# A planned order of work on one core, searched anew with measured costs, and its last weight loads without gates

## The chip, the core and the metric

The kernel runs on one core of a Trainium2 chip. The core has a matrix engine (TensorE, in the profile PE, with its weight loader PEld), a vector engine (VectorE, DVE), an activation engine (ScalarE, ACT), a general engine (GpSimd, POOL) and a sync engine (SyncE, SP), which here only issues transfers; 16 DMA engines carry them out. The metric is the device time of one execution in microseconds (us); less is better.

## The reference

Two residual blocks are applied to x (2048 tokens x 576, bf16), and then the same two again with the same weights:

```python
x = x + A(layernorm(x))     # attention in segments, with a memory
x = x + B(layernorm(x))     # silu(x @ w1) * (x @ w3) @ w2, 576 -> 4608 -> 576
x = x + A(layernorm(x))
x = x + B(layernorm(x))
```

A goes through 64 segments of 32 tokens one after the other:

```python
for s in range(64):
    h = concat([mem, xs])                   # 8 memory rows and 32 tokens: 40 x 576
    q, k, v = h @ Wq, h @ Wk, h @ Wv        # 32 heads of 128
    p = softmax(mask(q @ k.T * 128 ** -0.5))
    o = (p @ v) @ Wo                        # 40 x 576
    mem = o[:8]                             # the memory of the next segment
    outs.append(o[8:])
```

Segment s + 1 needs the first 8 rows of the output of segment s. This chain runs through all 64 segments in both layers.

## The kernel before, in words

**Steps.** Layer 1 runs 8 segments behind layer 0 (LAG = 8). The work falls into 72 steps: step t is segment t of layer 0 together with segment t - 8 of layer 1. In steps 8 to 63 both layers are there, and since they share the weights, one product serves both with 80 moving columns (2 x 40). In steps 0 to 7 and 64 to 71 only one layer is there, and the same product moves 40 columns. The feed-forward of a layer works on 4 segments (128 tokens) at a time, and its pieces are spread between the attention of the steps; for the last 4 segments of layer 1 it can only come after step 71.

**Pieces.** The work is cut into nodes. A node is a function that issues some instructions on one engine, with a cost (`dur`), a delay until its result can be read (`lat`), the nodes that it depends on (`deps`) and the buffers that it takes and gives back (`acq`, `rel`). `make_nodes` (L248) writes them all. The nodes of PE have a letter for each kind:

| letter | node | letter | node |
|---|---|---|---|
| Q, q | Q and K projection of some heads: main part (512 rows), tail (64 rows) | n, a, b | transposes of a layernorm's result |
| S | scores of 8 heads | p | POST: transposes attention's output back |
| T | transpose of the probabilities on PE (one-layer steps only) | F, f | feed-forward up (w1, w3): main, tail |
| P | probabilities times V | W, w | feed-forward down (w2), layer 0 and layer 1 |
| O, o | product with Wo: main, tail | V, v, X, x, G, g | value projections |
| m | transpose of the first memory | | |

For a group of 8 heads the chain is: Q, q; copies of the projection to QKT (L662 on ACT or L665 on DVE); S; on DVE and ACT mask, maximum, exponential and sum (SME, STAT); scaling into PB; the transpose to PTS; P; copy to OT; O, o. There are four such groups in a step. In steps with both layers the transpose from PB to PTS isn't done by PE but by a DMA that SP issues (node TR, `ptr_dma`, L1103, the rows `PTS<-PB`). In steps with one layer PE transposes (T) into a bank, and ACT or DVE copies the bank to PTS. There is one buffer of PTS, two of PB and of SME, four of QKT, eight banks.

**What sets the order.** PE's order is a string of letters that is written into the kernel: ORDER = FIRST + FOUR * 11 + LAST (L217 to L240), 3601 letters. FIRST holds steps 0 to 15, FOUR (208 letters) four steps with both layers, repeated eleven times, and LAST the rest. Each letter takes the next node of its kind. The order on the other engines (ACT, DVE, POOL, and SP's issues) comes from `plan` (L93 on): it goes through time with the nodes' costs, and whenever an engine is free it takes the ready node of the lowest `prio`. Evictions (kind AD) go to ACT or DVE, whichever the plan has free. The plan runs while the kernel is built; the chip only sees the result, a fixed order of instructions on each engine, and semaphores. A wrong cost in the plan can't break a dependency; it can put work in a poor place.

**Array modes.** PE runs a product on the whole array, on halves of rows or of columns, or on smaller parts. A node can permit several modes (`mode="full/col"`), and the plan chooses one so that the shape changes seldom. The helper `mm` (L659) issues a product in mode "col" as two products of 64 columns each.

**Loads.** All attention weights are in SBUF: W (Wq and Wk), WV, WO. Loads go out on SP (`dma`, L668), some small ones on ACT (`adma`, L671) and POOL (`swdma`, L674). Feed-forward weights come in pairs of pieces as they are used: W13 (two buffers) and W2C (two buffers). For the feed-forward behind step 71 there is another way: as soon as the last projections and values have been computed, W and WV are free, and `tail_load` (L741) puts the feed-forward weights into them, eight loads, each in two parts (one into W, 1.18 MB, one into WV, 0.59 MB). Loads 1 to 7 have a **gate** (L572): load 1 goes out only when PE has done O of group 1 in step 71, loads 2 to 7 only after O of group 3.

```python
gates = {1: me["WO1"], **{i: me[f"WO{NG - 1}"] for i in range(2, 8)}}
for i in range(8):
    g = gates.get(i)
    tail.append([load("tail", kb(128, c), s0 + o.tail_at + 0.01 * i, em.tail_load(i, what, g), deps=dep + [g])
                 for what, c, dep in ((0, 9 * 512, qk_done[i]), (1, 4 * 576, v_done))])
```

**Tiles that the change touches.** HT (L1355) holds the transposed input of a step, 128 partitions x 3 x 5 x 176 columns; YTS (L1368) holds attention's output for POST, 2 x 5 x 128 columns.

Of the kernel before, what the change touches and what calls it, by code (L numbers as in the profile page):

```python
# [33 lines left out]
PTR = 112  # L34

# [7 lines left out]
         "xr": 3, "xn": 2, "w13": 2, "w2": 2, "htt": 4}  # L43
# [14 lines left out]
def role(t):  # L58

    return (t - LAG) % 2  # L60
# [29 lines left out]
KINDS = {"m0tr": "m", "L0tr": "a", "L1tr": "b", "POST": "p", "Ftr": "n", "QK": "Q", "QKt": "q", "SC": "S", "TR": "T", "PV": "P",  # L90
# [121 lines left out]
def ewh(*ns):  # L212
# [5 lines left out]
    "maQqSQQvqqVSxXTqSPQSTOPXoTPOTPoOoOoQqqQvSSqVqQSQTPSTOPOToPToxPOOooQqqQSqvSaVQQSqTPSTPOOoTPoTPOOooQqqQSQSvqVQTSqX"  # L218
    "SPTPOTOPoToxPOOooQqqpQvSSVqnQfFSTFfqQPWSTOPFTOfPFTofoPOOooWQFfqqfFSQQSqqfFvVfTFSPQWTSFPXffOTFPOTOPWOooooaxQqqQSW"
    "FSQvfqTVfSFPQFTfqOPSWTOPFOTffoooPFOoWQqqvSQQSFfqVfSTWqFQFSPTfPOTWPoTOPOOooobQpvVqqqQQSnQqfxFSXqqfFQQQPSWFqqfQOfS"  # L220
# [6 lines left out]
    "QqqqqQppQQvVSSnnQFfqqQFqSfQQPFfqOwPoSWFffOPFWOowoPFOoFffqqQQQQqqWSwFSGgfqqQQQPQqqgWSSGFPFffggGGPwOFOPOOffooowoFv"  # L227
    "VqqqQQQWSFqfqqQQQSwWFPSFfqqfQQPwOSWFFPoffOOWPwOoooFfqqQQWaSqqQQQbSQqgqGSQPQqqgGSOPoGggOPGwOPooOo"
# [4 lines left out]
    "QPFSTOPofFTOPwTWPOOoooFfqfqQQSQSFvqfVfqFTQPSWwSTFPxXffTFPOOTWOPwOFooooFqffqQQSWwVvqfSQFfqTQPSWTwPOSFOTfFPwTOPWOo"  # L233
    "oooFqfqfFQQWSfqSFwvVQQTSqffPWwSTFFPOoTOWPoTwPOOoobQpqxqvVSnQXqfFSQTQSPFfqOoTSFfPTwPOOoofTFPFOowQfqqQSQSFvqfVTqfF"
    "PQTSwPSXffFTOOPwTOPFOooooFxqfQQqqSvVSQTQSFPfqfOTSPwoOTFPFTOPoofOowQQfqqFSSvVqQQSqTwPTSPOOFTofPTPOOooopfffFFFnwfw"
    "FFffFFwfFffFwffwFFFFffwFwfffFFFwffFFwfffFFww"
# [11 lines left out]
def make_nodes(em, nseg, pools, o=Opt, dma_bw=230e3, load_bw=345e3):  # L248
# [24 lines left out]
    def load(name, nbytes, prio, fn, deps=()):  # L273
        return node("DMA", nbytes / load_bw, fn, deps=deps, prio=prio, name=name, lat=2.0)

    ld_m0 = node("ACT", 0.1, em.load_m0(), prio=-90, name="m0", lat=2.5)
    ld_t = [load("ldt", kb(3 * R64, 4096), -10.0, em.load_tails(0)), node("ACT", 0.1, em.load_tails(1), prio=-120, name="ldt", lat=6.0)]
# [47 lines left out]
    vx_ev, last_v, pvs = {}, [], {}  # L325

    def v_nodes(name, t, k, prio, tail_at, emit, strips, deps, tail_deps, free):

# [1108 lines left out]
```

## Time and profile before

| | |
|---|---|
| median of 3 runs | 2654.93 us (2654.26 to 2665.12) |
| the profiled execution's own time | 2657.81 us |
| its span (first to last recorded instruction) | 2656.0 us |
| TensorE busy | 2578.3 us, 97% |
| VectorE, ScalarE, GpSimd busy | 75%, 47%, 13% |
| mean granted TensorE clock | 0.992 |
| DMA packets | 371.48 MB, mean 140 GB/s |
| largest group of matmuls | bank<-HT,W, 785.1 us, 23,040 of them |

The profile is of one execution. Rows of groups read: line, engine, operation, what it writes <- what it reads, partitions x elements and type, how many; after the first bar the busy time in us and the mean of one in ns; after the second the engine's idle time just ahead of them and what ended most of it. Rows of waits read: engine, tile and line that waited, what it waited for; then the total in us, how often, and the longest. Rows of the queue of SP read: start in us, length, queue, line, what is loaded, and how many were joined in the row. Since most instructions are issued by a few helpers (L659, L662, L665, L668), they are told apart by their tiles.

### The profile page before, as it was taken

The page shows a single profiled execution, that of the slowest core. Times are in us where ns is not written, and L with a number is a line of the kernel's source. Part 1 is how long each engine was busy: PE and PEld are TensorE (multiplying, and loading weights), DVE is VectorE, ACT ScalarE, POOL GpSimd, SP SyncE. Part 2 cuts the span into 40 slices and gives each one's busy share as a digit, 9 for nine tenths or more (in the row PEclk, how much of TensorE's full clock was granted, in tenths as well). Part 3 has the DMA queues.
Part 4 walks back from the last instruction along what each step waited for, and adds up shares of the span by engine and source line. Part 5 has one row for each costly group of instructions (what it writes and reads, how often), then busy time and mean ns, then how long its engine had stood idle before and what let it go on. Part 6 is the DMA issues. An engine that isn't in the chain of part 4 may idle for free.

```text
span 2656.0 us, 133410 instructions
## 1 busy us (share of the span) xinstructions
PE 2578.3 (97%) x59426; PEld 2216.6 (83%) x59426; DVE 2004.1 (75%) x5137; ACT 1242.3 (47%) x3495; POOL 335.2 (13%) x399
## 2 busy tenths in 40 slices
PE   6899999999999999999999999999999999999998
PEld 4788878888888888888888888888888888888887
DVE  4677777877787778778777877877787787777866
ACT  2555453444545444454544544454444445454443
POOL 1111111110101111010101101110110111011110
PEclk8899999999999999999999999999999999999999
DMA  9055746556554655555465555645565554554458
GB/s 322 4 153 150 182 101 152 128 131 157 117 141 108 152 135 126 155 128 139 109 143 134 138 146 125 146 106 151 122 147 139 132 140 106 129 139 131 130 155 244
DMA packets 690433, 371.48 MB, mean 140 GB/s; under 512 B 234328, under 2 KB 682592, under 8 KB 689216
## 3 DMA queue, kind: packets, MB, share of 16 engines
q1 hardware_dynamic: 686320, 355.08, 53.5%
q8 instruction: 464, 7.60, 1.2%
q0 software_dynamic: 3024, 6.93, 0.9%
q10 hardware_dynamic: 512, 0.94, 0.2%
q14 instruction: 113, 0.93, 0.1%
HBM read 306.72 MB, written 2.36 MB: 116 GB/s over the span
## 4 chain that ended last, share of the span: by engine, by line
PE 83%; DMA 9%; DVE 5%; ACT 1%; issue 1%; SPq 1%; POOL 0%; ACTq 0%; DVEq 0%; POOLq 0%
PE bank L659 83%; DMA PTS<-PB 5%; DMA W<-in_B_w_dram 1%; DMA W2C<-in_B_w_dram 1%; DVE STAT L665 1%; DMA WV<-in_A_Wv_dram 1%; DVE SME L665 1%; DVE PB L665 1%; SPq L668 1%; DVE V L665 0%; DMA W<-in_A_Wq_dram 0%; ACT V L662 0%; DVE XR L665 0%; DVE HTT L665 0%; DVE LNS L665 0%
## 5 line engine op out<-in xcount | busy, mean ns | idle before, releaser
L659 PEld LDWEIGHTS <-W 128*128 128x128 bf16 (+2 forms) x32464 | 1259.9, 100 | 118.1 <-issue 63.6
L659 PE MATMUL bank<-HT,W 128*128 128x80 bf16 (+3 forms) x23040 | 785.1, 197 | 16.1 <-issue 9.3
L659 PE MATMUL bank<-XTB,W 128*64 128x256 bf16 (+5 forms) x9424 | 658.9, 263 | 2.0 <-DMA W<-in_B_w_dram 2.0
L1093 POOL MEMSET PB<- 128x1024 bf16 x288 | 273.9, 951 | 1944.4 <-DMA PTS<-PB 1142.8
L662 ACT ACTIVATE QKT<-bank 128x256 bf16<-128x256 f32 (+4 forms) x1423 | 342.4, 320 | 246.4 <-PE bank L659 216.9
L659 PE MATMUL bank<-OT,WO 128*128 128x80 bf16 (+3 forms) x11520 | 421.2, 199 | 1.0 <-ACT OT L662 0.5
L662 ACT ACTIVATE V<-bank 64x512 bf16<-64x512 f32 (+1 forms) x605 | 339.6, 585 | 164.9 <-PE bank L659 158.4
L659 PEld LDWEIGHTS <-WO 128*128 128x128 bf16 (+1 forms) x11520 | 387.8, 102 | 34.0 <-issue 18.7
L659 PE MATMUL bank<-WV,HT 128*32 128x512 bf16 (+4 forms) x3768 | 370.4, 386 | 5.1 <-DMA WV<-in_A_Wv_dram 4.5
L659 PE MATMUL bank<-W2C,HTT 128*64 128x288 bf16 (+1 forms) x3216 | 321.8, 287 | 3.4 <-DMA W2C<-in_B_w_dram 2.8
L662 ACT ACTIVATE OT<-bank 128x320 bf16<-128x320 f32 x374 | 153.8, 437 | 313.2 <-PE bank L659 309.3
L665 DVE TENSOR_REDUCE STAT<-SME 104x8 f32<-104x320 f32 (+1 forms) x576 | 275.1, 478 | 27.9 <-ACT SME L662 22.3
L665 DVE TENSOR_TENSOR PB<-SME,STAT 40x128 bf16<-40x128 f32 (+4 forms) x912 | 275.4, 336 | 12.1 <-DVE STAT L665 0.4
L665 DVE SCALAR_TENSOR_TENSOR HTT<-HTT,bank 128x512 bf16<-128x512 bf16 (+1 forms) x324 | 201.5, 622 | 106.7 <-ACT HTT L662 103.7
L659 PEld LDWEIGHTS <-HT 128*32 128x32 bf16 (+4 forms) x3768 | 155.4, 100 | 145.2 <-issue 39.1
L659 PEld LDWEIGHTS <-HTT 128*64 128x64 bf16 (+1 forms) x3288 | 230.1, 105 | 40.8 <-issue 7.3
L662 ACT ACTIVATE HTT<-bank 128x512 bf16<-128x512 f32 (+1 forms) x324 | 173.9, 548 | 179.9 <-PE bank L659 178.3
L665 DVE SCALAR_TENSOR_TENSOR XR<-bank,XR 128x288 f32<-128x288 f32 x574 | 241.5, 447 | 14.4 <-PE bank L659 11.0
L662 ACT ACTIVATE SME<-SME 104x320 f32<-104x320 f32 (+1 forms) x288 | 135.1, 469 | 241.4 <-DVE SME L665 238.1
L665 DVE TENSOR_TENSOR HTT<-HTT,bank 128x512 bf16<-128x512 bf16 (+1 forms) x324 | 203.7, 629 | 33.0 <-PE bank L659 0.5
L665 DVE CAST QKT<-bank 128x192 bf16<-128x192 f32 (+2 forms) x497 | 141.4, 328 | 104.7 <-PE bank L659 102.5
L665 DVE CAST V<-bank 64x512 bf16<-64x512 f32 (+1 forms) x259 | 177.3, 684 | 36.9 <-PE bank L659 33.0
(60 smaller groups left out, 1394.4 us busy)
## 6 DMA issues: line engine op xcount, KB each, us to landing
W<-in_B_w_dram SPq DMA_DIRECT2D x608, 256.0 KB, 3.9
W2C<-in_B_w_dram SPq DMA_DIRECT2D x304, 288.0 KB, 3.5
W<-in_B_w_dram SPq DMA_DIRECT2D x608, 32.0 KB, 3.9
W<-in_B_w_dram SPq DMA_DIRECT2D x16, 512.0 KB, 8.3
WO<-in_A_Wo_dram SPq DMA_DIRECT2D x4, 1152.0 KB, 10.0
XR<-in_A_x_dram POOLq DMA_DIRECT2D x16, 288.0 KB, 4.0
WV<-in_B_w_dram SPq DMA_DIRECT2D x8, 576.0 KB, 7.3
W<-in_A_Wq_dram SPq DMA_DIRECT2D x16, 256.0 KB, 5.8
```

What stands on the lines that cost most here:

```text
L659: self.ch("PE", self.nc.tensor.matmul(out, lhsT=lhsT, rhs=rhs, start=start, stop=stop, skip_group_check=True, **k))
L662: self.ch("ACT", self.nc.scalar.activation(*a, **k))
L665: self.ch("DVE", getattr(self.nc.vector, fn_)(*a, **k))
L668: self.ch("SP", self.nc.sync.dma_start(out=out, in_=in_))
L1093: return lambda n: self.ch("POOL", self.nc.gpsimd.memset(self.T.PB[:, pb.i, 0:GROUPS[g][1]], 0.0))
```

## The change

It does five things.

1. **Costs.** The planner's costs get new values: the rate at which the first weights load goes from 345 to 380 GB/s, and the last weights get a rate of their own, 330; the first small loads take 9 to 12 us in place of 2.5 to 6; the scaling into PB takes 1.04 or 0.97 us in place of 1.34 or 1.17 (0.46 in a step with one layer); the delay of the DMA transpose is 2.3 in place of 2.45 us; tails, sums, multiplications and W13 loads become a little longer, scores and values a little shorter.
2. **Order.** FIRST, FOUR and LAST are new strings, with the same number of letters of each kind. From letter 257 to the end of FIRST, and for the first 269 letters behind the last FOUR, they are the same as before.
3. **Gates.** GATES is empty: the eight loads behind step 71 depend only on the projections and values that last read W and WV.
4. **Tiles.** HT has 184 columns in place of 176 (the last 8 aren't used here). YTS has 9 blocks of 128 columns in place of 2 x 5: the 64-row tails of both layers share one block, layer 0 on partitions 0 to 63 and layer 1 on 64 to 127, and POST transposes accordingly.
5. **Unused code.** New functions (`ahead`, `xq`, `xq_ev`, `xq_store`, `xq_load`, `qk_rhs`, `stage`) could compute projections of some segments ahead. PRE is empty, so none of their nodes is made, and `qk_rhs` returns what `qk` used before.

The string that is repeated eleven times, before (-) and after (+); FIRST and LAST differ in the same manner in their early and late parts:

```diff
 FOUR = (
-    "QqqqqQppQQvVSSnnQFfqqQFqSfQQPFfqOwPoSWFffOPFWOowoPFOoFffqqQQQQqqWSwFSGgfqqQQQPQqqgWSSGFPFffggGGPwOFOPOOffooowoFv"
-    "VqqqQQQWSFqfqqQQQSwWFPSFfqqfQQPwOSWFFPoffOOWPwOoooFfqqQQWaSqqQQQbSQqgqGSQPQqqgGSOPoGggOPGwOPooOo"
+    "QqqqqQppQQVvSnSnQFfqqQFSfqQQPFfqOwPSWFoffPOFWOwPFOoooFffqqQQWQQqqSwFSGfqgqQQQPQgqSGfqfFPFWSGggOPGwOFPOOooowoFqff"
+    "vVQQQqqqWSFfqqQQQSWawFSPFfqqfQQOPWSwFFPffOOwPWOooooFqfqQQWqqSQQQSbQQgqqqGSQPqgGOSPgGgOPGwOPoooOo"
 )
```

The first letters (step 0 and the start of step 1) and the last ones (from the last O of step 71 on):

```diff
 FIRST = (
-    "maQqSQQvqqVSxXTqSPQSTOPXoTPOTPoOoOoQqqQvSSqVqQSQTPSTOPOToPToxPOOooQqqQ
+    "maqQQQSqSXvxqTVPSTqQPSOTXPOOToooxPOoQqQSqqqSQQvSSTVPTPTOPoOTOPooOoQqqQ
...
 LAST = (
...
-SPOOFTofPTPOOooopfffFFFnwfw" "FFffFFwfFffFwffwFFFFffwFwfffFFFwffFFwfffFFww"
+SPTPOOTOPffTfoPOOoopFFfFnwFw" "fffFFFwffFFwffFFwfffFFwFwfffFFFwffFFwfffFFww"
```

The core of the rest:

```diff
+PRE = ()
+GATES = {}
...
-def make_nodes(em, nseg, pools, o=Opt, dma_bw=230e3, load_bw=345e3):
+def make_nodes(em, nseg, pools, o=Opt, dma_bw=230e3, load_bw=380e3, tail_bw=330e3):
...
-            w = 0.168 * (4 - e if nl == 2 else 2) + nl * w40 / 960
+            w = (1.04 - 0.07 * e if nl == 2 else 0.46) * nh / 8
             pbs = node("DVE", w, em.sm_pb(t, g, sme, pb), deps=[d], prio=pf, acq=[pb], rel=[sme], name="pb")
...
-                tr = node("DMA", 1.27 * nh / 8, em.ptr_dma(t, g, pb, pts), deps=[pbs], prio=pf - 0.02, acq=[pts], name="TR", lat=2.45)
+                tr = node("DMA", 1.27 * nh / 8, em.ptr_dma(t, g, pb, pts), deps=[pbs], prio=pf - 0.02, acq=[pts], name="TR", lat=2.3)
...
-            gates = {1: me["WO1"], **{i: me[f"WO{NG - 1}"] for i in range(2, 8)}}
+            gates = {i: me[k] for i, k in GATES.items()}
...
-                tail.append([load("tail", kb(128, c), s0 + o.tail_at + 0.01 * i, em.tail_load(i, what, g), deps=dep + [g])
+                tail.append([load("tail", kb(128, c), s0 + o.tail_at + 0.01 * i, em.tail_load(i, what, g), deps=dep + [d for d in [g] if d])
                              for what, c, dep in ((0, 9 * 512, qk_done[i]), (1, 4 * 576, v_done))])
...
-    T.HT = sp.tile([P, R_HT // 2, 5, 2 * SW + 2 * MEM], BF, name="HT")
+    T.HT = sp.tile([P, R_HT // 2, 5, 2 * SW + 3 * MEM], BF, name="HT")
...
-    T.YTS = sp.tile([P, 2, 5, P], BF, name="YTS")
-    T.mem0T = T.YTS[:, 1, :, 0:MEM]
+    T.YTS = sp.tile([P, 9, P], BF, name="YTS")
+    T.mem0T = T.YTS[:, 5, 0:5 * MEM].rearrange("p (c m) -> p c m", c=5)
```

As built, after issues 59,118 matmuls in place of 59,426 (fewer products are split in two halves), 3458 activations on ACT in place of 3494 and 965 copies on DVE in place of 929 (36 evictions change engine). The number of transfers is the same. Behind step 70 SP issues in another order, where `t0w` is the part of load 0 that goes into W and `t0v` the one that goes into WV:

```
before  t0w  W13   t0v  W2C  W2C  t1w  t1v  t2w ...
after   t0w  t1w   t0v  W13  t1v  W2C  W2C  t2w  t2v ...
```

More of the change, by code (lines that the diff above doesn't have):

```diff
@@ L34 @@
 PTR = 112
+PRE = ()
+AHEAD = True
+BACK = 4
+GATES = {}
 TIED = True
@@ new lines, in stage, with xq, f @@
+    def stage(self, st):
+        if st.i < 4:
+            x, k = self.T.W13[:].rearrange("p a b c -> p (a b c)"), st.i
+        elif st.i < 6:
+            x, k = self.T.W2C[:].rearrange("p a b c -> p (a b c)"), st.i - 4
+        else:
+            x, k = self.T.HTT[:].rearrange("p a b c -> p (a b c)"), st.i - 6
+        return x[:, k * 1024:(k + 1) * 1024]
+    def xq(self, half, u, b, tail):
+        def f(n):
+            X = self.T.XTB[:, half]
+            first = self.begin(b)
+            for j in range(4):
+                e0 = (4 * u + j) * E
+                for kind in (0, 1):
+                    o = self.bk(b[kind])[:, j * P:(j + 1) * P]
+                    if tail:
+                        rr = slice(kind * R64, (kind + 1) * R64)
+                        self.mm(o, self.T.W[rr, 8, e0:e0 + E], X[rr, 4, :], first and j == 0, True, tile_position=(kind * R64, 0))
+                    else:
+                        for c in range(4):
+                            self.mm(o, self.T.W[:, 4 * kind + c, e0:e0 + E], X[:, c, :], first and j == 0 and c == 0, c == 3)
+        return f
```

155 lines of the change are left out of this document (110 added, 45 removed).

## The prediction

> **What bounds the kernel now.** I read the first page first: is one engine full, and is anything else near it?
>
> ```profile
> span 2656.0 us, 133410 instructions
> ...
> PE 2578.3 (97%) x59426; PEld 2216.6 (83%) x59426; DVE 2004.1 (75%) x5137; ACT 1242.3 (47%) x3495; POOL 335.2 (13%) x399
> ...
> q8 instruction: 464, 7.60, 1.2%
> ...
> PTS<-PB SPq DMA_TRANSPOSE x224, 3.1
> ```
>
> TensorE (PE) is busy in 2578.3 of 2656.0 us. The change alters neither the products nor their number, so all that a new order can win is the rest, 77.7 us, and the question is where it lies. I therefore cut the span at the ends of steps, read off the timeline: step 0 to 60, steps 1 to 7 to 237, steps 8 to 15 to 532, the eleven repeats of FOUR to 2227, then the end, with the last step (71) from 2586 to 2613 and the last feed-forward behind it. The columns are: stretch, its length, busy time of each engine, granted clock, DMA share, GB/s.
>
> ```profile
> 0.00:60.00 60.00, 37.49 (x755) 23.80 (x755) 25.53 (x58) 14.31 (x30) 10.16 (x22) 0.89 1.02 346
> 60.00:237.00 177.00, 162.16 (x5023) 140.94 (x5021) 128.27 (x339) 93.37 (x220) 29.56 (x33) 0.93 0.36 100
> 237.00:532.00 295.00, 287.49 (x6569) 243.29 (x6565) 229.98 (x603) 137.10 (x413) 35.87 (x42) 1.00 0.61 138
> 532.00:2227.00 1695.00, 1678.80 (x37078) 1455.33 (x37079) 1298.06 (x3322) 801.60 (x2345) 206.78 (x242) 1.00 0.56 134
> 2227.00:2586.00 359.00, 351.85 (x8733) 302.41 (x8732) 277.51 (x700) 174.06 (x434) 47.89 (x54) 1.00 0.50 133
> 2586.00:2613.00 27.00, 22.70 (x680) 19.53 (x680) 16.07 (x45) 12.20 (x29) 3.81 (x4) 0.94 0.67 197
> 2613.00:2656.00 43.00, 37.85 (x626) 31.26 (x620) 28.71 (x71) 9.69 (x25) 1.13 (x2) 1.00 0.89 272
> ```
>
> Length less PE's busy time gives its idle time by stage: 22.5, 14.8, 7.5, 16.2, 7.2, 4.3 and 5.2 us. The DMA share is 1.02 in the first stage and 0.89 in the last: there weights arrive as fast as they can. In between DMA stands at half and PE at 99%: 1695 us of FOUR hold only 16.2 idle us, 1.5 us a repeat.
>
> **The change part by part.** The sum is made against the profiled execution, 2657.81 us (its span and 1.8 us around it); the median shown is 2654.93, 2.9 less. I work out a difference and take it from the median.
>
> *The work itself.* Both letter strings hold 3601 letters with the same count of each letter. After issues 59118 matmuls, 308 fewer, because fewer groups are issued in two halves of 64 columns. Is a half cheaper?
>
> ```profile
> L659 PE MATMUL bank<-W2C,HTT 128*128 128x288 bf16 x1248 | 179.5, 287 | 2.2 <-DMA W2C<-in_B_w_dram 1.6 <-DVE HTT L665 0.5
> ...
> L659 PE MATMUL bank<-W2C,HTT 128*64 128x288 bf16 x1968 | 142.3, 287 | 1.2 <-DMA W2C<-in_B_w_dram 1.2
> ```
>
> Whole: 179.5 / 1248 = 0.144 us. In halves: 142.3 / (1968 / 2) = 0.145 us. So the 308 are worth nothing. The letters change the array's shape 1209 times in place of 1215 (66 times in a FOUR, in both). Six changes are worth between 0 and 1.7 us, if one costs at most the mean of the weight loader's unexplained gaps in FOUR, 91.2 / 322 = 0.28 us (row below). I take **-0.5**, near the low end, since those gaps hold other things too.
>
> *Step 0* (22.5 idle).
>
> ```profile
> PE bank L659 <- DMA XTB<-in_A_mem_dram: 10.0, 1, 10.0
> PE bank L659 <- DMA WV<-in_A_Wv_dram: 4.5, 3, 1.9
> PE bank L659 <- ACT PTS L662: 3.1, 3, 2.0
> ```
>
> The first loads are issued in the same order in both kernels, only the planner's guess of their arrival differs (380 for 345 GB/s, 9 for 2.5 us for the memory). So the 10.0 us ahead of the first matmul and the 4.5 us for WV stay. What can go is the 3.1 us of waits for PTS: the PE transposes a group's probabilities (T), ACT copies them out, and the PV product (P) reads the copy; where P stands right behind T, PE waits for the copy. Before has TP twice in step 0, after never. In exchange P now stands right behind V (VP), whose results must be copied out as well. I take **-2** (bounds -3.1, all of it, and +1, a new wait at VP as long as a mean one now).
>
> The Trainium skill (DMA: Bandwidth & Descriptors, Specifications) gives a core about 358 GB/s from HBM, which speaks against planning with 380.
>
> ```profile
> 20.00:30.00 10.00, 8.77 (x164) 5.70 (x159) 3.16 (x8) 0.91 (x2) 0.00 (x0) 1.00 1.04 397
> 30.00:40.00 10.00, 5.51 (x131) 2.81 (x126) 0.99 (x3) 1.29 (x3) 0.00 (x0) 0.79 1.01 405
> ```
>
> Here 397 and 405 GB/s were moved in two stretches of 10 us, above the plan's new rate. By the page's figure WV's 4.2 MB would take an estimated 1.2 us longer than at 400, and the term would be -0.8.
>
> *Steps 1 to 7* (14.8 idle).
>
> ```profile
> PE bank L659 <- issue: 4.2, 6, 1.4
> PE bank L659 <- ACT PTS L662: 3.6, 6, 0.9
> PE bank L659 <- ACT QKT L662: 1.6, 3, 1.2
> ```
>
> TP stands 6 times in before and 4 times in after: 2 x 3.6 / 6 = 1.2 us. The one scores group (S) of step 1 that stood 1.2 us behind its projection's copy (QKT) now has a projection between: 0.8 of it goes. Step 1 gains one VP: +0.6. I take **-1.4** (bounds -5 and +3: the 4.2 us named issue have no cause in the profile and can fall anywhere).
>
> *Steps 8 to 15* (7.5 idle): from letter 257 to the first FOUR the letters are the same, only ACT's and DVE's shares of the copies differ. **0**, between -3 and +3.
>
> *FOUR, eleven times* (16.2 idle).
>
> ```profile
> PE bank L659 <- DMA PTS<-PB: 11.4, 18, 0.9
> PE bank L659 <- ACT HT L662: 3.8, 11, 0.3
> ...
> PEld L659 <- issue: 91.2, 322, 1.1
> ```
>
> The 3.8 us are one wait of 0.3 at the joint of two repeats: the string still ends in o and begins in Q, so it stays. The 11.4 us are 18 of 176 PV products that wait for the transpose of their probabilities, here a DMA. Which way does after move them? I count the letters between the k-th S and the k-th P of a FOUR. Before: 14.9 on average, shortest 11, 12, 12, 12. After: 14.4, shortest 10, 10, 10, 12. A letter is worth 1695 / (11 x 208) = 0.74 us, so cover shrinks by 0.3 us on average and by 0.7 to 1.5 at the tightest. It shrinks because the new costs make this chain shorter: the transpose from 1.27 + 2.45 to 1.27 + 2.3 us, the scaling of a group (PB) from 1.34 to 1.04. The rows allow the first, issue to landing has a median of 3.1, and are doubtful on the second:
>
> ```profile
> L665 DVE TENSOR_TENSOR PB<-SME,STAT 40x192 bf16<-40x192 f32 x368 | 128.6, 350 | 1.5
> ...
> L665 DVE TENSOR_TENSOR PB<-SME,STAT 40x128 bf16<-40x128 f32 x368 | 104.3, 284 | 6.2 <-DVE STAT L665 0.4
> ```
>
> Two of each make 2 x 0.350 + 2 x 0.284 = 1.27 us. If the 18 waits grow by 0.3 each, that is 5.4; if they are only shuffled, 0. I take **+3** (bounds -11.4, all gone, and +30, worked out below).
>
> *The end.* From 2227 the first 269 letters are the same; of the rest
>
> ```profile
> PE bank L659 <- issue: 4.8, 5, 2.0
> ...
> PE bank L659 <- ACT PTS L662: 0.9, 2, 0.6
> ...
> PE bank L659 <- DMA W<-in_B_w_dram: 1.0, 1, 1.0
> ```
>
> the first row is of 2227 to 2586: **-0.5** (-4 to +4, as with issue above). The second is of step 71: its one TP goes, **-0.9**. The third is all that PE waits for weights behind step 71, and the gates decide it. The queue of SP, the engine that issues the loads:
>
> ```profile
> 2588.45 7.24 SPq L668 DMA_DIRECT2D W<-in_B_w_dram  x8
> 2595.79 0.53 SPq L668 DMA_DIRECT2D WV<-in_B_w_dram  x1
> 2604.43 0.89 SPq L668 DMA_DIRECT2D W2C<-in_B_w_dram  x2
> 2608.01 2.89 SPq L668 DMA_DIRECT2D W<-in_B_w_dram  x4
> 2610.95 0.59 SPq L668 DMA_DIRECT2D WV<-in_B_w_dram  x1
> 2612.87 2.12 SPq L668 DMA_DIRECT2D W<-in_B_w_dram  x4
> ```
>
> ```profile
> 2620.00:2630.00 10.00, 10.00 (x165) 8.52 (x160) 6.43 (x16) 3.25 (x8) 0.58 (x1) 1.00 1.09 345
> ```
>
> Load 0 goes out at 2588. Then SP waits for a W2C buffer until 2604.43, for the gate of load 1 until 2608.01, for the gate of load 2 until 2612.87. Without gates the 2.7 us from 2605.3 and the 1.3 us from 2611.5 go, and load 1 (1.77 MB) now stands ahead of the W2C wait: at 345 GB/s 5.1 us of transfer more. All later loads land some 9 us sooner (2.7 + 1.3 + 5.1), and PE, which waits 1.0 us for the last, no longer waits: **-1.0**. Late next is PE itself, 37.85 us busy of 43. Against it: the last pair of W13 is now queued behind both parts of load 0 and the first of load 1, and its product (f) stands ahead of the last PVs of step 71; up to +1.5 if it lands late.
>
> The sum: -0.5 - 2 - 1.4 + 0 + 3 - 0.5 - 0.9 - 1.0 = **-3.3 us**. 2654.93 - 3.3 = 2651.6, said as **2652 us**.
>
> **The rivals.**
>
> *Slower: FOUR's transposes miss.* Place: the three P at 10 letters in each FOUR. Price: if each waits as long as the longest wait now, 0.9, that is 3 x 11 x 0.9 = 30 us, less at most the 11.4 there now; +18 to +30, say +24 in place of +3: 2673. It decides once a landing takes over a microsecond longer than 3.1. For it: after's cover is shorter; the waits now come back at the same letter every third FOUR, as the chain of waits shows, where the same piece begins each time a wait ends:
>
> ```profile
> 805.97 35.17 PE bank L659 x776
> ...
> 1267.29 35.17 PE bank L659 x776
> ...
> 1729.03 35.17 PE bank L659 x776
> ```
>
> 461.3 us are three FOURs. Instructions come in 464 pieces, so one holds 59426 / 464 = 128 matmuls with their weight loads. A FOUR has 3370 matmuls, 26.33 pieces; three have 79. So I read these waits as transposes that travel beside an instruction fetch. After's FOUR has 3338, 26.08 pieces: its fetches would move slowly through the letters, and a wait should come back in several FOURs running, then stop. Against it: 158 of 176 do not wait now.
> The Trainium skill (DMA: Bandwidth & Descriptors, Queues, rings and completion order) says that a DMA engine drains a whole packet of one queue before it turns to the next, which would hold a transpose up behind an instruction packet; no row here times a single packet.
>
> *Faster: the search found what the old costs hid.* Half of the idle time from 60 us on, and 5 us of step 0: -5 - 7.4 - 8.1 - 3.6 - 2.2 - 1 = -27, so 2628. For it: the old costs let PE start at 2.5 us where it starts at 10, so the old order was searched on a wrong clock. Against it: most of that idle is not named by a wait that the letters remove.
>
> *The change does not do what it says.* Real waits, on buffers still read and on W still in use, hold SP as the gates did, and the shuffle cancels: 2654.
>
> *A wider HT.* Most products that read HT stand in one row:
>
> ```profile
> L659 PE MATMUL bank<-HT,W 128*128 128x80 bf16 (+3 forms) x23040 | 785.1, 197 | 16.1 <-issue 9.3
> ```
>
> Its tile grows from 176 to 184 columns a piece. If that slowed its readers by 1 ns each it would be +23, 2678; nothing in the profile prices it.
>
> **How the numbers follow.** Forecast 0.52 (own range 2640 to 2664), change without effect 0.12, faster 0.19, slower by FOUR 0.13, by HT 0.04. About 0.5% (13 us) is what a measurement of this kernel can tell from no change. Faster by more: 0.19 and a little of the forecast, 0.20. Slower by more: 0.13 and most of 0.04, 0.16. Within: 0.64. The range 2630 to 2672 holds the first two and most of the next two.
>
> **What would show it.** In after: PE busy within 3 us of 2578; waits for PTS copies down from 12 to about 7; waits for the DMA transposes in FOUR between 10 and 20 us, in runs of neighbouring FOURs; no PE wait for W behind step 71, and SP's last W load ahead of 2635. It is wrong if PE's busy time moves, if the gain sits in FOUR, or if PE still waits for the last loads.

## The result

The changed kernel takes 2670.35 us (median of 7 runs, 2661.52 to 2672.84) against 2654.93 (7 runs, 2652.43 to 2665.12). The ratio is 1.0042, 95% interval 1.0025 to 1.0059: it is slower by about 0.4%, where a gain of 0.1% was forecast. The forecast range, 2630 to 2672, holds the time; the direction was wrong. The profiled execution of the changed kernel took 2670.46 us.

The first page of the changed kernel's profile:

```profile
span 2668.7 us, 132801 instructions
...
PE 2572.8 (96%) x59063; PEld 2215.6 (83%) x59118; DVE 2035.2 (76%) x5173; ACT 1221.5 (46%) x3459; POOL 335.5 (13%) x399
...
q8 instruction: 462, 7.57, 1.2%
```

The work did not grow. 55 matmul records are missing here (59,063 of 59,118); a trace of the same products without gaps (the first experiment) has PE busy for 2579.8 us, against 2578.3 before. So the time is idle time again, and the stretches between the ends of steps say where. They are cut at this kernel's own step ends (columns as in the prediction):

```profile
0.00:60.60 60.60, 34.63 (x733) 22.42 (x736) 26.38 (x60) 13.32 (x28) 9.51 (x21) 0.92 1.00 337
60.60:234.70 174.10, 159.58 (x4971) 138.77 (x4971) 129.31 (x342) 92.23 (x217) 30.01 (x34) 0.96 0.36 103
234.70:530.80 296.10, 288.25 (x6559) 243.82 (x6564) 230.56 (x601) 137.53 (x415) 35.96 (x42) 1.00 0.59 138
530.80:2233.50 1702.70, 1676.36 (x36674) 1454.15 (x36718) 1323.66 (x3344) 784.40 (x2321) 207.09 (x242) 1.00 0.56 134
2233.50:2384.70 151.20, 149.40 (x3291) 129.91 (x3296) 118.81 (x308) 66.85 (x190) 18.22 (x21) 1.00 0.56 135
2384.70:2595.80 211.10, 203.30 (x5527) 174.27 (x5522) 161.44 (x403) 105.03 (x235) 29.74 (x33) 0.98 0.45 129
2595.80:2624.60 28.80, 23.51 (x705) 20.26 (x701) 15.80 (x44) 12.24 (x28) 3.81 (x4) 0.94 0.86 253
```

The second column is the length. Set beside the same steps of the kernel before (read off its timeline in the same way; the last row ends at PE's last matmul):

| stretch | before | after | difference | forecast |
|---|---|---|---|---|
| step 0 | 60.1 | 60.6 | +0.5 | -2 |
| steps 1 to 7 | 176.9 | 174.0 | -2.9 | -1.4 |
| steps 8 to 15 | 295.2 | 296.1 | +0.9 | 0 |
| FOUR, eleven times | 1694.4 | 1702.7 | +8.3 | +3 |
| steps 60 to 63 | 149.8 | 151.2 | +1.4 | -0.5 for both |
| steps 64 to 70 | 209.9 | 211.1 | +1.2 | |
| step 71 | 27.0 | 28.8 | +1.8 | -0.9 |
| last feed-forward | 39.3 | 40.6 | +1.3 | -1.0 |
| sum | 2652.6 | 2665.2 | +12.6 | -3.3 with -0.5 for the array's shape |

Two places hold the miss: FOUR, and everything behind it. First the end. PE's waits of the changed kernel behind step 70 (from 2595.8 us):

```profile
PE bank L701 <- issue: 7.2, 5, 3.0
PE bank L701 <- DVE YTS L707: 0.8, 1, 0.8
```

and the row that stands there before (from 2586.3 us):

```profile
PE bank L659 <- issue: 3.3, 3, 2.0
```

Both waits that the prediction removed are gone: PE no longer waits for W, nor for a copy of PTS. In their place "issue", time in which PE waits for nothing that the profile names, grew from 3.3 to 7.2 us. The chain of work that ended last shows where (start, length):

```profile
2604.42 4.25 PE bank L701 x127
2608.67 3.02 issue
...
2622.20 2.45 PE bank L701 x91
...
2626.64 2.05 issue
2628.69 3.36 PE bank L701 x58
```

PE runs 127 matmuls, stands for 3 us, goes on, and stands again. At the same time SP's queue does what the change wanted:

```profile
2599.36 6.15 SPq L710 DMA_DIRECT2D W<-in_B_w_dram  x8
2605.71 0.44 SPq L710 DMA_DIRECT2D WV<-in_B_w_dram  x1
2607.51 3.53 SPq L710 DMA_DIRECT2D W<-in_B_w_dram  x4
...
2617.61 3.26 SPq L710 DMA_DIRECT2D W<-in_B_w_dram  x4
...
2642.41 4.88 SPq L710 DMA_DIRECT2D W<-in_B_w_dram  x4
```

Loads 0 and 1 go out together, 2.4 MB in 6 us, during step 71. Counted from the end of step 71, the last load into W goes out at +17.8 us where it was +25.0 (2638.28 - 2613.3): counted so the loads are 7 us sooner, and the end is later. (In time from the start of the kernel the last load goes out at 2642.41, later than before, since step 71 itself ends 11.3 us later.)

**What the unnamed waits are.** PE's instructions reach it by DMA, in packets of 16 KB (the row q8: 7.57 MB in 462 packets; here a packet is one such record of the profile, and what PE gets by it, 256 instructions, is called a piece). I counted PE's instructions in program order (matmuls, weight loads and the few others) and put the waits on that count. In the fourteen traces of this case PE stands still for over 0.8 us 72 times behind 2400 us. Of these, 71 stand at position 194 or 195 of 256 and end 1.2 to 1.7 us (median 1.4) after such a packet; the 72nd is the wait of the kernel before for its last W. So PE stops where a new piece of 256 instructions begins. The fetch of the next piece starts about when PE enters the last one that it has, as the delays below show. So PE stands for

delay until the packet starts + time of the packet + about 1.4 us (1.2 to 1.7) - time that PE needs for a piece.

Worked out from the records of the changed kernel (us; "delay" is from PE's entry into a piece to the start of the next packet; four of the pieces are shown; "PE stands" is counted from the start of the last matmul to the start of the next, which is 0.2 to 0.4 us more than the idle time in the profile's rows):

```
PE enters a piece   delay   packet   + resume   piece lasts   PE stands
2599.58             2.12    1.24     1.48       4.29          0.55
2604.42             4.62    1.22     1.43       4.07          3.20
2622.20             4.05    1.14     1.30       4.21          2.27
2628.69             4.33    1.14     -          7.22          0
```

In FOUR the delay is 0.4 us in the kernel before and 0.5 in the changed one (medians), and a piece lasts 5.6 us: 0.4 + 1.04 + 1.4 is far below that, and PE does not stop. With one layer a piece mostly lasts 3.5 to 5 us, and a delay of 2 to 4 us is enough to stop PE. In the last feed-forward a piece lasts 7 to 9 us, and the same delay of 4 us costs nothing.

**FOUR.** PE's waits in the eleven repeats, after:

```profile
PE bank L701 <- DMA PTS<-PB: 12.8, 16, 2.0
PE bank L701 <- ACT HT L704: 3.8, 11, 0.3
PE bank L701 <- issue: 3.5, 22, 0.2
PE bank L701 <- DVE V L707: 1.9, 9, 0.3
PE bank L701 <- DMA W2C<-in_B_w_dram: 1.3, 2, 0.7
PE bank L701 <- DMA W<-in_B_w_dram: 1.0, 2, 0.8
PE bank L701 <- DVE QKT L707: 0.7, 2, 0.4
```

The 22 issue waits are two missing matmul records a repeat; a trace without missing records has none of them. The waits for the transposes grew a little, and came as forecast, in neighbouring repeats: behind letter 40 in repeats 0 to 3, behind 99 in 6 and 7, behind 155 in 0 to 2 (letters and repeats are counted from 0, here and below). Below them stand rows that the prediction did not have: a copy of V, W2C, W, QKT. To sum by letter, I took from each of the 208 letters the shortest of its eleven times as its own time and the rest as waiting. The own times sum to 152.2 us a repeat before and 152.3 after (the wider HT costs nothing); waiting is 19.7 us before and 27.8 after. Ahead of a P it is 16.7 and 18.9; ahead of the value projection behind letter 95, 0 and 3.1; ahead of a q behind a W, 0.2 and 3.2.

### The profile page after: what moved, and what is told of

Same layout as the page of the kernel before. It is cut to its first block, busy times and chain, and to the rows that moved or that the text cites. A ratio compares the mean times of both kernels' runs of the same rounds, so it can differ in the third digit from the quotient of the medians.

```text
span 2668.7 us, 132801 instructions
## 1 busy us (share of the span) xinstructions
PE 2572.8 (96%) x59063; PEld 2215.6 (83%) x59118; DVE 2035.2 (76%) x5173; ACT 1221.5 (46%) x3459; POOL 335.5 (13%) x399
## 3 DMA queue, kind: packets, MB, share of 16 engines
q8 instruction: 462, 7.57, 1.2%
## 4 chain that ended last, share of the span: by engine, by line
PE 76%; DVE 13%; DMA 7%; issue 2%; ACT 1%; SPq 0%; POOL 0%; ACTq 0%; DVEq 0%; POOLq 0%
PE bank L701 76%; DMA PTS<-PB 5%; DVE STAT L707 2%; DVE HTT L707 2%; DVE SME L707 2%; DVE V L707 2%; DVE PB L707 2%; DVE QKT L707 1%; DMA WV<-in_A_Wv_dram 1%; DMA W2C<-in_B_w_dram 1%; DVE XR L707 1%; DVE LNS L707 1%; DMA W<-in_A_Wq_dram 0%; DVE OT L707 0%; DMA W<-in_B_w_dram 0%
## 5 line engine op out<-in xcount | busy, mean ns | idle before, releaser
L704 ACT ACTIVATE QKT<-bank 128x64 bf16<-128x64 f32 (+4 forms) x1457 | 345.9, 316 | 283.8 <-PE bank L701 278.3
L701 PE MATMUL bank<-OT,WO 128*128 128x80 bf16 (+3 forms) x11520 | 410.9, 198 | 3.0 <-issue 2.2
L704 ACT ACTIVATE V<-bank 32x512 bf16<-32x512 f32 (+1 forms) x595 | 335.2, 584 | 144.0 <-PE bank L701 136.6
L701 PE MATMUL bank<-WV,HT 128*32 128x512 bf16 (+4 forms) x3627 | 364.0, 386 | 10.2 <-issue 4.1
L704 ACT ACTIVATE OT<-bank 128x320 bf16<-128x320 f32 x323 | 136.4, 437 | 321.5 <-PE bank L701 317.4
L701 PEld LDWEIGHTS <-HT 128*32 128x32 bf16 (+5 forms) x3680 | 156.6, 100 | 142.6 <-issue 41.4
L704 ACT ACTIVATE HTT<-bank 128x512 bf16<-128x512 f32 (+1 forms) x324 | 174.0, 548 | 204.3 <-PE bank L701 202.1
L707 DVE CAST QKT<-bank 128x128 bf16<-128x128 f32 (+2 forms) x463 | 132.9, 330 | 96.2 <-PE bank L701 93.1
L707 DVE CAST V<-bank 64x512 bf16<-64x512 f32 (+1 forms) x269 | 184.5, 686 | 24.3 <-PE bank L701 19.2
```

The lines of the kernel that those rows point to most:

```text
L701: self.ch("PE", self.nc.tensor.matmul(out, lhsT=lhsT, rhs=rhs, start=start, stop=stop, skip_group_check=True, **k))
L704: self.ch("ACT", self.nc.scalar.activation(*a, **k))
L707: self.ch("DVE", getattr(self.nc.vector, fn_)(*a, **k))
```

## The experiments

Theory at the start: (1) the loads without gates make PE's instructions late; (2) FOUR's new letters lose what FOUR lost. Rivals: the last step's new letters cost the end; the new costs, which place the copies, cost FOUR. Lengths in the table are from each profile, in us; the ratio is to the kernel before in the same session.

| kernel | median | ratio (95%) | FOUR | 60 to 63 | 64 to 70 | 71 and behind |
|---|---|---|---|---|---|---|
| before | 2654.93 | 1 | 1694.4 | 149.8 | 209.9 | 66.3 |
| after | 2670.35 | 1.0042 (1.0025 to 1.0059) | 1702.7 | 151.2 | 211.1 | 69.4 |
| after, old gates | 2667.46 | 1.0041 (1.0023 to 1.0059) | 1704.5 | 151.9 | 212.5 | 66.1 |
| before, no gates | 2658.84 | 1.0007 (0.9994 to 1.002) | 1692.2 | 150.4 | 208.8 | 68.6 |
| after, old FOUR | 2675.91 | 1.0075 (1.0054 to 1.0095) | 1712.5 | 151.8 | 209.0 | 65.6 |
| before, new FOUR | 2666.77 | 1.0038 (1.0025 to 1.0051) | 1705.2 | 150.0 | 206.4 | 64.6 |
| after, locked, 42 ahead | 2664.00 | 1.0021 (1.0007 to 1.0036) | 1695.9 | 151.8 | 212.6 | 68.3 |
| after, locked, 6 ahead | 2680.81 | 1.0084 (1.0057 to 1.0112) | 1715.2 | 152.6 | 211.1 | 64.0 |
| after, 64 ahead | 2673.66 | 1.0060 (1.0043 to 1.0077) | 1701.6 | 150.7 | 211.0 | 67.2 |
| after, letters exchanged | 2670.31 | 1.0058 (1.0041 to 1.0075) | 1704.0 | 151.9 | 211.0 | 67.1 |
| before, locked, 8 ahead | 2652.50 | 0.9982 (0.9970 to 0.9993) | 1691.7 | 149.6 | 208.8 | 66.0 |
| before, locked, 48 ahead | 2655.39 | 0.9991 (0.9977 to 1.0005) | 1695.8 | 150.7 | 206.2 | 62.5 |

### The gates

In the changed kernel, the old gates:

```diff
-GATES = {}
+GATES = {1: "WO1", 2: "WO3", 3: "WO3", 4: "WO3", 5: "WO3", 6: "WO3", 7: "WO3"}
```

> The changed kernel with the old gates back on the last eight loads, all else as it is. Theory 'fetch': PE stops where the next 16 KB of its instructions come late, and the loads that now go out during step 71 are what makes them late. Then, from the end of step 70 on, PE's waits named issue fall from 7.8 us (0.9, 3.2, 1.4, 2.3) to about 3.5, the wait for the last W returns with about 1, and the end is 2 to 3 us shorter: 2667 to 2668. Rival 'letters': the new letters of the last step cost it, the gates nothing; then that stretch stays within 1 us, 2670, or is longer by the W wait. The stage of FOUR should stay as it is (154.8 us a repeat), since nothing in it changes.

In the kernel before, none:

```diff
-            gates = {1: me["WO1"], **{i: me[f"WO{NG - 1}"] for i in range(2, 8)}}
+            gates = {}
...
-                tail.append([load("tail", kb(128, c), s0 + o.tail_at + 0.01 * i, em.tail_load(i, what, g), deps=dep + [g])
+                tail.append([load("tail", kb(128, c), s0 + o.tail_at + 0.01 * i, em.tail_load(i, what, g), deps=dep + [d for d in [g] if d])
```

> The kernel before with its gates taken off, order and costs as they were. Theory 'fetch': the waits named issue behind step 70 rise from 3.5 us to 6 or more, the wait for the last W (1.0 to 1.2 us) goes, and the sum is 1 to 3 us slower, 2656 to 2658. Rival 'gates only delay': the W wait goes and nothing comes in its place, 1 us faster, 2654. FOUR stays at 154.0 us a repeat.

Waits behind step 70, first of the changed kernel with the old gates, then of the kernel before without them:

```profile
PE bank L701 <- issue: 4.4, 4, 1.8
```

```profile
PE bank L659 <- issue: 5.5, 3, 2.1
```

7.2 becomes 4.4 with gates, 3.3 becomes 5.5 without. Step 71 and what is behind it go from 69.4 to 66.1, and from 66.3 to 68.6: 3.3 us and 2.3 us, as the theory said, where the rivals had 0 or 1 the other way. The wait for the last W did not come back in the changed kernel with gates; I had expected it. The times themselves can't tell: 2 to 3 us are 0.1%, less than their intervals, so only the traces can. In the kernel before they do. Two more traces with the same end, gates and place in the instruction stream took 66.5 and 66.6 us, with 4.6 and 4.2 us of issue (the kernels with extra loads, below); without gates they are 68.6 and 5.5. In the changed kernel the size is less sure: a second trace of its end, without gates and with as many instructions ahead of it (letters exchanged, below), took 67.1 us with 5.7 us of issue. So the loads without gates cost 2.0 to 2.3 us in the kernel before, and 1.0 to 3.3 in the changed one.

### Letters against costs

Each kernel with the other's FOUR, all else its own (the diff is that of FOUR in the change, one way and the other).

> The changed kernel with the old string for the eleven repeats of four steps (new costs, new first and last strings). Theory 'letters of FOUR': the 8 us lost between step 15 and step 59 are in the new string; a repeat takes 154.0 us again, 1694.5 for eleven, 8 less in all: 2662. Rival 'costs': the loss is in which engine copies what, which the new costs decide; a repeat stays at 154.8 and the time at 2670.

> The kernel before (old costs, old first and last strings, gates) with the new string for the eleven repeats. Theory 'letters of FOUR': a repeat takes 154.8 us, 8 us more in all: 2663. Rival 'costs': a repeat stays at 154.0, 2655. Either way PE waits for the DMA transposes at the same letter in neighbouring repeats, three or four in a row, because a repeat now holds 26.1 pieces of instructions, and no longer in every third.

Both theories fall in the simple form. The new letters cost about 11 us under the old costs (1705.2 for 1694.4; four traces with the old letters and costs took 1691.8 to 1697.4), so they do carry a loss. But the old letters under the new costs are the slowest of all, 1712.5. The waits of that kernel in FOUR:

```profile
PE bank L701 <- DVE XR L707: 7.7, 11, 0.7
PE bank L701 <- DMA PTS<-PB: 4.2, 10, 0.8
...
PE bank L701 <- ACT OT L704: 2.6, 11, 0.2
```

PE waits for XR and for OT in each of the eleven repeats at the same place. XR is an addition, which the plan leaves on DVE under either set of costs, and OT a copy, here on ACT. That the new costs let the plan place both later than the old letters need them is argued from these rows; no run moved one of them alone. What the runs do show is that this order of letters and the costs that it was searched with belong together: half of either loses. In the other hybrid the new letters wait for the transposes as in the changed kernel (14.1 us in 21 waits, the longest 2.2) and not at all for the copy of V: that wait comes only with the new costs. So does the loss in steps 60 to 63, whose letters are the same in both strings: 149.6 to 150.7 in the five traces with the old costs above, 150.7 to 152.6 in the seven with the new.

### Fetches at fixed letters

If the waits for the transposes come from instruction packets that travel at the same time, a FOUR of exactly 26 pieces meets them at the same letters in all eleven repeats, and a few small matmuls at the very start, where PE has nothing to do, choose the letters.

```diff
     seq = [next(its[c]) for c in letters]
+    for r in range(11):
+        for p in (184, 193):
+            seq[len(FIRST) + len(FOUR) * r + p].mode = ["full"]
...
+            for _ in range(42):
+                self.mm(self.bk(b)[:, 0:32], self.T.ident[:, 0:P], self.T.ident[:, 0:32], True, True)
             for c in range(5):
                 c0 = min(c * P, D - P)
...
+            for _ in range(4 if t in range(16, 60, 4) and uh == 0 else 0):
+                x, w = self.qk_rhs(t, slice(0, P), 0)
+                self.mm(self.bk(b[0])[:, 0:w], self.T.W[:, 0, 0:E], x, True, True)
```

> The changed kernel with FOUR made exactly 26 pieces of 256 instructions long (6655 in place of 6680: in each repeat one value projection and one PV product are issued whole instead of in halves, and four copies of the first matmul are added), and 42 small extra matmuls ahead of the first transpose, where PE waits for its first load. So every repeat meets the instruction fetches at the same letters. By the two traces of these letters, repeats that began 126 to 150 instructions behind a piece's end lost 1.4 to 1.7 us, those at 54 to 78 lost 3.7. This kernel puts all eleven at 126 to 137. Theory 'fetch': FOUR takes 11 x (152.3 + 0.2 + 1.5) = 1694 us, 9 less than the changed kernel, waits come back in all repeats or in none. Rival 'fetches do not matter': 1703 + 2 for the switches of array mode, whatever the place.

The twin has 6 in place of 42.

> The same kernel with 6 extra matmuls ahead in place of 42, so that every repeat begins 54 to 65 instructions behind a piece's end; nothing else differs. Theory 'fetch': FOUR takes 11 x (152.5 + 3.7) = 1718 us, 24 more than its twin with 42. Rival 'fetches do not matter': within 2 us of the twin.

Waits for the transposes in FOUR, with 42 and with 6:

```profile
PE bank L704 <- DMA PTS<-PB: 5.2, 9, 1.7
```

```profile
PE bank L704 <- DMA PTS<-PB: 23.4, 23, 1.7
```

36 small matmuls, executed while PE waits for its first load, move FOUR by 19.3 us (1695.9 and 1715.2; 24 were expected) and the medians by 16.8. With 6 ahead, the P behind letter 40 waits at least 1.0 us and the one behind 155 at least 0.7 in all eleven repeats. Nothing else differs between the two, so the place decides these waits. That it does so by the packets, the transposes themselves show, in FOUR of seven traces: 284 of them with no instruction packet near (none that starts between 1.3 us before and 3.6 behind their issue) took 2.96 us from issue to landing (median), 95% of them under 3.5; 179 with a packet that starts 0.75 to 2.25 us behind their issue took at least 3.4, median 4.3. A transpose that lands a microsecond late makes its product wait.

The same for the kernel before (letters 49, 50, 87 and 88 whole, 8 ahead, then 48):

> The kernel before, its costs, letters and gates, with FOUR made exactly 26 pieces of 256 instructions long (6656 in place of 6744: two feed-forward groups and two PV products in each repeat are issued whole instead of in halves, four copies of a first matmul are added) and 8 small extra matmuls ahead of the first transpose, which puts the fetches where repeats 2, 5 and 8 of the kernel before had them; these lost 0.7 us where the mean lost 1.8. Theory 'fetch': FOUR takes 11 x (152.2 + 0.2 + 0.7) = 1684 us or a little less, 9 less than before, and the time is 2646: faster than both kernels. Rival 'chance of single repeats': FOUR stays at 1693 or, by two more switches of array mode a repeat, 1696.

> The same kernel with 48 small extra matmuls ahead in place of 8, which puts the fetches where repeats 0, 1, 4 and 7 of the kernel before had them (1.0 us at one letter and up to 1.0 at one or two more). Theory 'fetch': FOUR takes 11 x (152.4 + 2.0) = 1698 us, some 14 more than its twin. Rival: within 2 us of the twin.

```profile
PE bank L662 <- DMA PTS<-PB: 4.6, 16, 0.6
```

```profile
PE bank L662 <- DMA PTS<-PB: 11.6, 14, 1.2
```

Again the waits go the way that was expected, but the gain is small: 1691.7 and 1695.8 us, where 1684 and 1698 were expected. With 8 ahead, the four added matmuls and one more change of shape cost 0.3 us a repeat, the P behind letters 76 and 184 wait 0.2 us a repeat on average, and the rest of the waiting is 1.0 us a repeat where 0.7 was expected. With 48 ahead the P behind letter 198 waits 0.7 to 1.2 in every repeat. Only the waits show the effect here: 1691.7 and 1695.8 us are no further apart than four traces of one and the same FOUR (1691.8 to 1697.4, with the letters and costs of the kernel before). With 8 ahead the kernel is faster than both kernels of the case: 0.9982, interval 0.9970 to 0.9993. That this gain comes from the place is not shown, since the interval of the twin with 48 ahead, 0.9977 to 1.0005, overlaps it.

### The same end at other places

```diff
+            for _ in range(64):
+                self.mm(self.bk(b)[:, 0:32], self.T.ident[:, 0:P], self.T.ident[:, 0:32], True, True)
```

> The changed kernel with 64 small extra matmuls (128 instructions, half a piece) ahead of the first transpose, where PE waits for its first load; nothing else differs. Theory 'fetch': all long waits named issue again stand where PE begins a new piece of 256 instructions, so they move to other matmuls; step 71 and the end behind it, 69.4 us, change by some us, up or down by chance of the place (65.6 was measured for the same letters with other instructions ahead); FOUR, which wanders through the places anyway, stays at 1703, give or take 3. Rival 'the new letters of the last steps cost it': step 71 and the end stay at 69.4 within 1.

FOUR stayed (1701.6). Step 71 and behind went from 69.4 to 67.2, with the long waits again at the starts of pieces and at other matmuls. With new costs, new letters at the end and no gates in all of them, this stretch took 64.0 to 69.4 us. Not all of that is the place: the kernel with letters exchanged has the same end with as many instructions ahead of it as the changed kernel and took 67.1, so some 2.3 us differ from one execution to the next. A part of the loss at the end of the changed kernel was therefore chance, as large as the gates' own 1 to 3 us.

### Loads that feed nothing

72 extra loads in steps 1 to 3 of the kernel before, into buffers that are still unused, four in flight at a time:

```diff
+            if t in (1, 2, 3) and uh == 0:
+                x = self.T.W13[:].rearrange("p a b c -> p (a b c)").rearrange("p (s h d) -> p s h d", s=4, h=2)
+                for k in range(24):
+                    self.dma(x[:, k % 4], self.a.wo[2 * k % 32:2 * k % 32 + 2].rearrange("h e d -> e h d"))
```

> The kernel before with 72 extra loads of 0.29 MB (21 MB, of Wo, into W13's buffers while these are still unused) on SP's queue in steps 1 to 3; they feed nothing. Theory 'fetch': while they run, the next piece of PE's instructions comes later than PE needs it (a piece lasts 3 to 4.4 us there); PE's waits named issue in steps 1 to 4 rise from 0.3 us to over 8, each at the start of a piece. Rival 'PE's own sequencer is what stops it in dense stretches': no change in these waits, only some on the loads themselves.

And with two in flight (k % 2):

> The kernel before with the 72 extra loads in steps 1 to 3, now only two in flight at a time in place of four (0.6 MB in place of 1.2). With four, an instruction fetch began 1.0 to 2.5 us after PE had crossed into its last fetched piece, against 0.1 to 1.0 without the loads; the loads of the last steps, with more in flight, made it 4.0 to 4.6. Theory 'queue': the fetch waits behind the bytes that are in flight ahead of it; with two it begins 0.5 to 1.5 us after. Rival 'busy engines': any load that keeps the engines busy delays it as much; 1.0 to 2.5 again.

The first expectation failed in its size. From 110 to 125 us DMA moved 261 GB/s, and 167 with two in flight, against 5 without (the kernel before, then four, then two):

```profile
110.00:125.00 15.00, 13.65 (x443) 10.94 (x438) 12.35 (x32) 8.97 (x20) 2.19 (x3) 0.96 0.02 5
```

```profile
110.00:125.00 15.00, 12.32 (x377) 10.27 (x371) 12.01 (x33) 9.32 (x23) 2.85 (x3) 0.78 0.87 261
```

```profile
110.00:125.00 15.00, 14.43 (x457) 12.23 (x455) 9.71 (x24) 7.96 (x21) 1.90 (x2) 0.77 0.61 167
```

The delay of an instruction packet (median of 14 to 18 packets in these steps) was 0.6 us without the loads (0.1 to 1.1), 1.0 with two in flight (0.2 to 1.8), 1.5 with four (1.0 to 2.5); in the changed kernel's step 71 and behind the median is 4.1. With four, PE stood at the starts of pieces three times, 0.2 to 0.6 us, where it did not before. By the formula a delay of 2.2 us with pieces of 4 us makes about that; 8 us needed the delay of the last steps, which these loads did not reach. So extra loads do delay the packets, and with more in flight the median grows, though the ranges overlap. What counts, bytes in flight or the busy share of the DMA engines (0.02, 0.61, 0.87), the runs leave open, since both rose together. (Both kernels take longer as a whole, 2682.88 us with four in flight and 2715.95 with two, one run each, for another reason: the next x tile waits behind the extra loads on SP, and DVE waits for it, 20.9 us with four.) The Trainium skill (DMA: Bandwidth & Descriptors, Queues, rings and completion order) has each DMA engine go round its queues packet by packet, by which an instruction packet would wait for one packet of each other queue and no more. That the delay grew from 1.0 to 1.5 us with the same loads, twice as many in flight, speaks against a fixed wait. One record of these loads (1152 bytes) took 0.05 us (median), far less than the delay; whether what the section calls a packet is one such record or several, no run here shows.

### A copy that the plan made too short

```diff
-GfqfFPFWSGggOPGwOFPOO
+GfqfFPFWSGggOGPwOFPOO
```

> The changed kernel with two neighbouring letters of FOUR exchanged: the PV product that reads the last value projection's copy (letter 95, ggOPG) goes behind the next value projection (ggOGP). The number of instructions stays, so the fetches keep their places. In the plan the copy on DVE takes 0.6 us and ends 0.19 us ahead of that product; in the trace of the changed kernel such a copy takes 0.685, and PE waits for it in 9 of 11 repeats, 3.1 us ahead of the value projection behind and up to 0.8 more. Theory 'packed too close': these waits go, and FOUR takes 1699 us in place of 1703. Rival 'the wait moves': with P later, O and the next step come later too, and FOUR stays at 1703.

The copies of V, by form, in the changed kernel (ACT, then DVE; busy, mean ns):

```profile
L704 ACT ACTIVATE V<-bank 64x512 bf16<-64x512 f32 x295 | 165.4, 584 | 88.8 <-PE bank L701 86.9
L707 DVE CAST V<-bank 64x512 bf16<-64x512 f32 x153 | 104.8, 685 | 13.1 <-PE bank L701 11.0
```

The change did not touch this cost: 0.6 us on DVE where it takes 0.685, and the search left 0.19 us between the copy and the product. The rival won: the waits for V are gone from FOUR, but FOUR took 1704.0, not 1699. The work behind it now waits 0.3 us in every repeat for the copy of this product's result (OT), and W2C waits rose from 1.3 to 2.9 us. A wait at one place of a full order is not worth its length.

## Why the prediction was wrong

**The end.** The step that failed: "Without gates the 2.7 us from 2605.3 and the 1.3 us from 2611.5 go [...] PE, which waits 1.0 us for the last, no longer waits: -1.0". The wait did go. But I priced the loads only by when they land, and not by what else they delay. The earlier loads come during step 71, where a piece of PE's instructions lasts 4 us, and put its packets 4 us late. In place of the forecast gain of 1.0 that costs 1 to 3 us (both gate experiments). "Late next is PE itself" was right in name and missed that PE's own instructions are a transfer. The row was there: "issue: 4.8, 5, 2.0" and, for steps 1 to 7, "4.2, 6, 1.4", of which I wrote that they "have no cause in the profile". They are the same waits, and two of the page's rows together name them: 464 packets, one for each 128 matmuls.

**FOUR.** The step that failed: the term +3 priced the waits for the transposes alone ("If the 18 waits grow by 0.3 each, that is 5.4; if they are only shuffled, 0") and put every other wait of a new order at nothing. The sign was right and the size a third: +8.3 measured. In traces with this FOUR and these costs it took 1701.6 to 1704.5 us (three), with the old pair 1691.8 to 1697.4 (four): 4 to 13 more. The part that I had worked out, the P behind the transposes, is +2.2 in the profiled pair (16.7 to 18.9 us by letter; up to +6.5 against the trace without gates), about the 0 to 5.4 of the working. Their pattern came as written, in runs of neighbouring repeats; the locks show the cause that I had only read from three equal stretches. What I left out is that new costs also move copies between ACT and DVE inside FOUR; I had counted these 36 moved copies, and priced none. Behind letter 95 PE waits +3.1 for the copy of V, with the new letters and new costs together and in no trace with the old costs. Behind a W it waits +3.0; the profile names a load of W2C there in two repeats and a copy of QKT in two, and the kernel before without gates has such waits too, so these are not shown to be moved copies. The sums by letter also don't say what FOUR would take without a wait: exchanging two letters took V's away, and FOUR was no shorter. So why the new pair takes 8 us more than the old one stays in part open. The rival "FOUR's transposes miss" needed the three P with the shortest cover to wait in every repeat; the kernel with 6 ahead comes near it, with two P that do, and takes +21.

**Steps 60 to 70.** -0.5 forecast, +2.6 measured. For 60 to 63, where "the first 269 letters are the same", I took the same letters for the same time. They are not: the copies sit elsewhere (+1.4; over the traces above 150.1 on average with old costs, 151.7 with new). From 2400 to 2590 us PE's idle time at the starts of pieces sums to 4.9 before and 5.9 after; what the rest is, no run separates.

**Step 0.** The waits for PTS went from 3.1 to 0, as forecast. The 2 us did not come, since others came in their place:

```profile
PE bank L701 <- DMA W<-in_A_Wk_dram: 3.5, 3, 1.5
PE bank L701 <- DVE QKT L707: 2.2, 2, 1.6
...
PE bank L701 <- ACT HT L704: 1.9, 1, 1.9
PE bank L701 <- DVE V L707: 0.9, 1, 0.9
```

Before, the first two were 1.8 and 1.2. In this stage, with the DMA engines busy throughout (share 1.00), the new order changed what PE waits for and not how long the stage took.

**Right:** the work itself (own times 152.2 and 152.3), steps 8 to 15 (+0.9 for 0), steps 1 to 7 in sign (-2.9 for -1.4; over all traces above, steps 0 to 7 together end at 235.9 us with the old strings and 233.8 with the new), a wider HT that costs nothing, the waits for copies of PTS (from 12 to 6, about 7 forecast), and SP free of gates. The sum of the measured terms, +12.6, is 0.47% of the span; the ratio of the runs is 0.42%.

**What stays open.** Runs of one kernel spread over up to 17.5 us (the kernel before: 2648.35 to 2665.88 in one session), and a stage such as steps 8 to 15 took 292.9 to 302.7 us in traces of equal work; no trace says why. The part of steps 64 to 70 named above and the split of FOUR's loss stay open too.

## What to carry to other kernels

A wait that the profile calls "issue" has a place in the engine's instruction stream: count the instructions, and if it stands where a new 16 KB piece begins and ends just behind such a packet, the engine's own code is the transfer that is late. A gate on loads that nothing waits for yet may be there to keep them away from such a stretch, so before it is taken off, look at what PE does while they fly, not only at when they land. And an order that was searched with one set of costs need not hold under another; compare costs with the rows of the trace for every operation that stands close to its reader, and expect a few us of chance from where the pieces fall.

## What the runs showed of the hardware

- PE's instructions come in packets of 16 KB, 256 instructions, 1.04 us each (median), and where PE has stopped for one it goes on 1.2 to 1.7 us after the packet's end (median 1.4). A piece of 40-column matmuls lasts 3.2 us at full granted clock (25 ns a matmul, 128 of them); 3.2 - 1.04 - 1.4 leaves 0.8 us for any delay. A piece in FOUR lasts 5.6 us (median).
- A transpose by DMA took 2.96 us from issue to landing (median of 284) with no instruction packet near it, and 4.3 (median of 179, none under 3.4) where a packet started 0.75 to 2.25 us behind its issue.
- 36 matmuls of 32 columns, executed in idle time at the start, changed the time of a 2.7 ms kernel by 0.6% (2664.0 and 2680.8 us).
